# Moving the block transposes of an attention kernel from the tensor engine to crossbar DMAs

## The chip, the cores and the metric

One core of a Trainium2 chip. The metric is the device time of one execution in microseconds (us). Engines are called PE (matmul), DVE, ACT, POOL (GpSimd) and SP (the sync engine, which here only issues DMAs). All inputs and the result are float32 in HBM; the kernel computes in fp16. Three terms of the profile: the *granted clock* is the share of its full clock that PE was given (1.00 is all of it); a DMA *lands* when its data has arrived, and its landing time runs from its issue to then; a *crossbar DMA* is one that transposes its data on the way (`dma_start_transpose`).

## The reference

Block-sparse attention for 8 batches, 8 heads, 576 positions and a head width of 64, followed by a two-layer feed-forward product over the 4608 rows that result.

```python
scores = (1 / sqrt(D)) * q @ k.T
mask_local   = (rel >= 0) & (rel < 32)                   # heads 0..3
mask_strided = (rel >= 0) & (col % 32 == row % 32)       # heads 4..7
attn = softmax(where(mask, scores, -1e9)) @ v
x = attn.transpose(0, 2, 1, 3).reshape(4608, 512)
h = x @ w_in                                             # 512 -> 2048
out = (max(h, 0) + alpha * min(h, 0)) @ w_out            # 2048 -> 512
```

q and k are drawn with a standard deviation of 0.1. The scores are therefore close to zero and the softmax is nearly flat.

## The kernel before

The feed-forward part runs in 9 chunks of 512 rows. Each chunk has 16 pieces of the first product and 16 of the second, each piece four matmuls of 128x512. Between these pieces the attention of a later batch is fed in small pieces, so that PE always has a big matmul to go on with. A batch has four pairs of heads: pairs 0 and 1 local, 2 and 3 strided. A "unit" is two pairs (u even: local, u odd: strided). A "step" g of the schedule holds the scores of pair g, the product with v of pair g-1 and the transposed result of pair g-2.

q, k and the results must be transposed, and before the change PE does it, block by block against an identity, with an eviction by DVE or ACT:

```python
def transpose_piece(u, nm):                     # q or k of a unit
    tp = pspool.tile([128, 8, 64, 2], F16, ...)
    for j in range(8):
        keep(nc.tensor.transpose(tp[:, j]..., blk, ident))
    ...                                         # evict, then 2 or 4 more for the last 64 rows
def x_piece(P):                                 # the result of a pair
    xp = pspool.tile([128, 1024], F16, ...)
    for t in range(P.n):
        keep(nc.tensor.transpose(xp[...], P.x16[0:P.w, 128*t : 128*t+128], ident[...]))
    if P.strided: keep(nc.scalar.copy(xT[:, P.hp, ...], xp...))
    else:         keep(nc.vector.tensor_copy(xT[:, P.hp, ...], xp[:, 0:576]))
# step g:  S(g,0)  P(g-1,0)  T(q)  X(g-2)  S(g,1)  P(g-1,1)  T(k)  [P(g-1,2)]
```

A chunk's first product reads `xT`, the transposed results, so it can't start before the last result of its batch is in place. The transposes of q and k are needed before the scores of their unit.

The softmax here doesn't subtract the row's maximum and nothing guards it: scores larger than these inputs give would overflow.

## Time and profile before

| | before |
|---|---|
| time, median (range) | 343.4 us (343.15 to 343.47) |
| span of the profiled run | 341.7 us |
| PE busy, mean granted clock | 329.2 us (96%), 1.00 |
| matmul instructions | 2733 |
| packets on the software (POOL) DMA queue | 41,920 |
| packets on the hardware (SP) DMA queue | 8,768 |
| wait of PE for `xT` | 2.0 us, six times |

The busy share of PE says that PE bounds; the wait of PE for `xT` says where a chunk meets the attention that feeds it.

### The profile page before, as it was taken

To read this page: it belongs to the slowest core of one execution; us is meant where nothing else is said; L and a number is where in the kernel's file an instruction comes from. 1 tells how busy PE (TensorE), PEld (TensorE's weight loads), DVE (VectorE), ACT (ScalarE), POOL (GpSimd) and SP (SyncE) were. 2 spreads that over 40 slices of the span, in tenths; PEclk is the share of its full clock that TensorE was granted. 3 is DMA by queue.
4 is the path that set the end of the run, shared out by engine and by line. 5 is a ranking of instruction groups with operands and counts; after the bars stand their busy time and mean duration, and the time that the engine had idled before them with its cause. 6 is when DMAs were issued, how large, how long until landed. Compare 5 with 4: busy or idle time off the path is not lost.

```text
span 341.7 us, 6741 instructions
## 1 busy us (share of the span) xinstructions
PE 329.2 (96%) x2733; PEld 172.2 (50%) x2733; DVE 193.1 (57%) x385; ACT 175.7 (51%) x315; POOL 147.7 (43%) x164
## 2 busy tenths in 40 slices
PE   6899999999999999999999999999999999999995
PEld 2554455445554455454558754445545454444444
DVE  3477825489546863488247844784368446704800
ACT  2645664376356744474448544763467326524611
POOL 7832495339887257644575429122611210000000
PEclk9999999999999999999999999999999999999999
DMA  7999999398696472746366084000100010011011
GB/s 231 172 206 207 245 209 184 81 283 113 105 119 182 71 49 70 221 69 45 72 186 106 6 95 77 31 2 32 63 31 2 33 62 32 2 61 61 2 61 62
DMA packets 50719, 33.67 MB, mean 99 GB/s; under 512 B 31984, under 2 KB 42368, under 8 KB 50688
## 3 DMA queue, kind: packets, MB, share of 16 engines
q0 software_dynamic: 41920, 17.37, 42.7%
q1 hardware_dynamic: 8768, 15.87, 13.0%
q8 instruction: 21, 0.34, 0.4%
q14 instruction: 10, 0.08, 0.1%
HBM read 38.01 MB, written 9.44 MB: 139 GB/s over the span
## 4 chain that ended last, share of the span: by engine, by line
PE 90%; ACT 3%; DVE 3%; DMA 1%; issue 1%; SPq 0%; ACTq 0%
PE hps L493 36%; PE ops L535 35%; PE sp L271 4%; PE pv L318 4%; PE tp L214 4%; PE xp L335 2%; DMA ql<-in_q_dram 1%; PE wps L557 1%; DVE x L327 1%; PE ops L526 1%; ACT xT L339 1%; ACT osb L540 1%; PE sp L287 1%; PE sph L287 1%; ACT kT L159 1%
## 5 line engine op out<-in xcount | busy, mean ns | idle before, releaser
L535 PE MATMUL ops<-wout,gT 128*128 128x512 f16 x560 | 138.8, 379 | 0.0
L493 PE MATMUL hps<-xT,win 128*128 128x512 f16 (+1 forms) x640 | 135.2, 358 | 2.3 <-ACT xT L339 2.0
L506 DVE SCALAR_TENSOR_TENSOR gT<-neg,oma,hps 128x512 f16<-128x512 f32 x144 | 106.0, 744 | 47.3 <-ACT neg L503 39.5
L503 ACT ACTIVATE neg<-hps 128x512 f32<-128x512 f32 x144 | 86.0, 597 | 45.2 <-PE hps L493 44.4
L305 POOL TENSOR_TENSOR et<-et,consts 128x576 f16<-128x576 f16 (+1 forms) x48 | 61.1, 1275 | 88.6 <-ACT et L295 88.5
L493 PEld LDWEIGHTS <-win 128*128 128x128 f16 x640 | 58.8, 98 | 56.6 <-issue 4.8
L535 PEld LDWEIGHTS <-gT 128*128 128x128 f16 x560 | 48.2, 98 | 43.8
L540 ACT COPY osb<-ops 128x512 f32<-128x512 f32 x35 | 20.5, 585 | 67.1 <-PE ops L535 61.0
L325 DVE RECIPROCAL rc<-pv 72x6 f32<-72x6 f32 (+2 forms) x80 | 14.9, 186 | 58.7 <-PE pv L318 58.6
L295 ACT ACTIVATE et<-sp 72x576 f16<-72x576 f32 (+1 forms) x56 | 36.2, 647 | 21.5 <-PE sp L271 13.2
L327 DVE TENSOR_TENSOR x<-pv,rc 72x384 f16<-72x384 f32 (+2 forms) x80 | 42.2, 527 | 2.7
L318 PEld LDWEIGHTS <-et 72*128 72x128 f16 (+1 forms) x448 | 22.9, 98 | 15.4 <-DVE x L327 1.1
L271 PEld LDWEIGHTS <-kT 64*128 64x128 f16 x448 | 10.8, 95 | 27.3 <-issue 19.5
L161 DVE COPY qT<-tp 128x1024 f16<-128x1024 f16 (+1 forms) x16 | 17.4, 1086 | 8.0 <-PE tp L214 8.0
L271 PE MATMUL sp<-qT,kT 64*128 64x72 f16 (+1 forms) x392 | 16.9, 201 | 2.0 <-ACT kT L159 1.9
L159 ACT COPY kT<-tp 128x1024 f16<-128x1024 f16 (+1 forms) x16 | 14.5, 905 | 8.1 <-PE tp L214 8.1
L557 PE MATMUL wps<-wrm 128*128 128x512 f16 x44 | 15.2, 416 | 1.2 <-DVE wrm L569 1.2
L151 POOL DMA_DIRECT2D vl<-in_v_dram x8 | 11.2, 1403 | 10.8 <-PE xp L335 8.9
L335 PEld LDWEIGHTS <-x 72*128 72x128 f16 (+1 forms) x224 | 11.8, 97 | 7.9 <-DVE x L327 2.0
L318 PE MATMUL pv<-vs,et 72*128 72x65 f16 x256 | 15.1, 194 | 0.1
L335 PE MATMUL xp<-consts,x 72*128 72x72 f16 (+1 forms) x224 | 13.7, 200 | 1.0 <-DVE x L327 0.9
L163 POOL COPY vs<-stv 72x1024 f16<-72x1024 f16 x14 | 14.2, 1035 | 0.0
(66 smaller groups left out, 186.8 us busy)
## 6 DMA issues: line engine op xcount, KB each, us to landing
out_dram<-osb SPq DMA_DIRECT2D x35, 256.0 KB, 2.0
ql<-in_q_dram SPq DMA_DIRECT2D x6, 512.0 KB, 5.7
kl<-in_k_dram SPq DMA_DIRECT2D x6, 512.0 KB, 6.6
stv<-in_v_dram POOLq DMA_DIRECT2D x8, 288.0 KB, 6.4
vl<-in_v_dram POOLq DMA_DIRECT2D x6, 384.0 KB, 6.9
win<-in_moe_w_in_dram POOLq DMA_DIRECT2D x4, 512.0 KB, 10.4
wout<-in_moe_w_out_dram POOLq DMA_DIRECT2D x4, 512.0 KB, 18.1
qs<-in_q_dram POOLq DMA_DIRECT2D x7, 256.0 KB, 4.2
```

The costliest lines, as they stand in the source:

```text
L271: keep(nc.tensor.matmul(sps[y][:, w * x : w * x + w], P.kT[hf, k0 : k0 + 128], P.qT[hf, w * t : w * t + w], start=(x == 0), stop=(x == len ...
L295: keep(nc.scalar.activation(ev.rearrange("r (y c) -> r y c", y=2), sp[0:r, :, 0:n], AF.Exp, scale=SCALE))
L305: keep(nc.gpsimd.tensor_tensor(ev, ev, m, op=ALU.mult))
L318: keep(nc.tensor.matmul(pv[:, 65 * x : 65 * x + 65], et[0:r, c : c + 128], v16[0:r, 2 * P.pr + hh, t, :] if P.strided else v16[:, 6 * (2 * ...
L327: keep(nc.vector.tensor_tensor(P.x16[0:w, c0 : c0 + 64 * nb].rearrange("r (c e) -> r c e", e=64), pvv[:, :, 0:64], rc[0:w, 0:nb].unsqueeze ...
L335: keep(nc.tensor.transpose(xp[:, P.w * t : P.w * t + P.w], P.x16[0 : P.w, 128 * t : 128 * t + 128], ident[0 : P.w, 0 : P.w]))
L493: keep(nc.tensor.matmul(hps[:, dst : dst + w], win16[:, kk, 128 * m : 128 * m + 128], xT[:, kk, src : src + w], start=(kk == 0 and x == 0) ...
L503: keep(nc.scalar.activation(neg, hps, AF.Relu, scale=-1.0))
L506: keep(nc.vector.scalar_tensor_tensor(gTs[n][:, m, :], neg, oma[:, m : m + 1], hps, op0=ALU.mult, op1=ALU.add))
L535: keep(nc.tensor.matmul(ops, gTs[n][:, kf, 128 * mt : 128 * mt + 128], wout16[:, kf, :], start=(kf == 0), stop=(kf == 15)))
L540: keep(nc.scalar.copy(osb, ops))
L557: keep(nc.tensor.matmul(wps, wrm[:, 0:128], wrm, start=True, stop=True))
```

## The change

Intent: PE is the bound, and the transposes are PE work. From batch 3 on (`DX = 3`) they go to crossbar DMAs on the SP queue. The q and k that those read have to lie in SBUF as fp16: for strided heads in 72 rows of 8 positions, for local heads as overlapping row blocks of 96 and 128 rows, loaded with a cast by POOL's DMA queue. Results of local pairs go straight into `xT`; those of strided pairs into `xs`, from which ACT copies them in place. The diff, cut to its core:

```diff
+    DX = 3
+    def load_d(b, strided):                       # POOL queue, float32 -> fp16
+        for nm, src in (("q", q), ("k", k)):
+            if strided: keep(nc.gpsimd.dma_start(qks[nm][0:72], ...))        # 1 KB runs
+            else:       keep(nc.gpsimd.dma_start(qkl[nm], bass.AP(...        # 128 B runs
+                    ap=[[D, n], [96 * D, 24], [1, D]])))
+    def transpose_d(u):                           # SP queue
+        for nm, dst in (("q", qTs[u % 2]), ("k", kTs[u % 2])):
+            keep(nc.sync.dma_start_transpose(o, qks[nm]... or qkl[nm]...))
+    def x_dma(P):                                 # SP queue
+        if P.strided: P.xs = xpool.tile([128, 8, 80], F16, ...)
+                      keep(nc.sync.dma_start_transpose(P.xs, P.x16[0:80, :]))
+        else:         keep(nc.sync.dma_start_transpose(xT[:, P.hp, ...], P.x16[0:96, 0:768]))
+    def x_copy(P):
+        keep(nc.scalar.copy(xT[:, P.hp, ...], P.xs[:, :, 0:72].rearrange("r t p -> r p t")))
...                                                # in step g, c = g // 4
-        okT = 8 <= t < npair and t % 2 == 0
+        okT = 8 <= t < 4 * DX and t % 2 == 0
-        if okX: seq.append(("X", X(x), x))
+        if 8 <= g - 2 < 4 * DX: seq.append(("X", X(g - 2)))
+                if i == 0:
+                    if g % 4 == 2 and DX <= c + 1 < B:
+                        transpose_d(2 * (c + 1))
+                    if g % 4 == 0 and DX <= c < B:
+                        transpose_d(2 * c + 1)
+                        if c + 1 < B:
+                            load_d(c + 1, False)
+                    if g % 4 == 2 and DX <= c and c + 1 < B:
+                        load_d(c + 1, True)
                 for b, pr in extra:                # steps g % 4 == 0: v of this batch
                     cast_v(b, pr, "pool")
                     if pr == 1 and b + 1 < B:
                         load_v(b + 1, True)
+                if lastp:                          # after the last product with v of the step
+                    if 4 * DX <= g - 1 < npair:
+                        x_dma(pairs[g - 1])
+                if copyp and ... pairs[g - 2].strided:    # at the second scores of the step
+                    x_copy(pairs[g - 2])
...
-                acc += left / (23.5 - 0.5 * skip) * ...
+                acc += left / (22.0 - 0.5 * skip) * ...
```

The old loads, casts and tail loads of batches 3 to 7 are gone. In step g = 4c the strided transposes of batch c, the row-block loads of batch c+1 and the strided load of v for batch c+1 are issued; in step g = 4c + 2 the local transposes of batch c+1 and its strided loads of q and k. At the end of each step g the result of pair g-1 is transposed: in step g = 4c the last result of batch c-1, which the next chunk waits for.

More of the change, by code (lines that the diff above doesn't have):

```diff
@@ L85 @@
     NE = 6
-    qTs = [cpool.tile([128, 2, S], F16, name=f"qT{i}") for i in range(2)]
-    kTs = [cpool.tile([128, 2, 672], F16, name=f"kT{i}") for i in range(2)]
+    DX = 3
+    qTs = [cpool.tile([128, 2, 672], F16, name=f"qT{i}") for i in range(2)]
+    kTs = [cpool.tile([128, 2, 768], F16, name=f"kT{i}") for i in range(2)]
     vls = [cpool.tile([128, 24, 65], F16, name=f"vl{i}") for i in range(2)]
@@ L90 @@
     ets = [cpool.tile([128, 640], F16, name=f"et{i}") for i in range(NE)]
+    qkl = {nm: cpool.tile([128 if nm == "k" else 96, 24, 64], F16, name=f"{nm}ld") for nm in "qk"}
+    mloc = cpool.tile([128, 576], F16)
+    x16s = [cpool.tile([80, 1024], F16, name=f"x16s{i}") for i in range(2)]
+    qks = {nm: cpool.tile([80, 4, 512], F16, name=f"{nm}sd") for nm in "qk"}
     loaded = {}
@@ L112, in load_qk @@
             ap=[[8 * D, 64], [2 * S * D, 2], [S * D, 2], [1, 8 * D]])))
+    def load_d(b, strided):
+        for nm, src in (("q", q), ("k", k)):
+            if strided:
+                keep(nc.gpsimd.dma_start(
+                    qks[nm][0:72], src[b, 4:8, :, :].rearrange("h (p t) d -> p h (t d)", t=8)))
+            else:
+                n = 128 if nm == "k" else 96
+                base = src[b, 0:1, 0:1, :]
+                keep(nc.gpsimd.dma_start(qkl[nm], bass.AP(
+                    tensor=base.tensor, offset=base.offset - (n - 96) * D,
+                    ap=[[D, n], [96 * D, 24], [1, D]])))
+    def transpose_d(u):
+        for nm, dst in (("q", qTs[u % 2]), ("k", kTs[u % 2])):
+            flat = dst.rearrange("r e c -> r (e c)")
+            if u % 2:
+                o = flat[:, 0:1280].rearrange("r (j p) -> r j p", p=80)
+                keep(nc.sync.dma_start_transpose(o, qks[nm].rearrange("p h c -> p (h c)")))
+            else:
+                n = 128 if nm == "k" else 96
+                o = flat[:, 0 : 12 * n].rearrange("r (j p) -> r j p", p=n)
+                keep(nc.sync.dma_start_transpose(o, qkl[nm].rearrange("r w d -> r (w d)")))
     def cast_s(b, nm, eng):
@@ L192, in make_pair @@
         u = g // 2
-        P.qT, P.kT = qTs[u % 2][:, g % 2], kTs[u % 2][:, g % 2]
+        P.dx = P.b >= DX
+        if P.dx:
+            P.qT, P.kT = (z[u % 2].rearrange("r e c -> r (e c)") for z in (qTs, kTs))
+        else:
+            P.qT, P.kT = qTs[u % 2][:, g % 2], kTs[u % 2][:, g % 2]
         P.sgroups = ([0, 1, 2, 3], [4, 5, 6, 7]) if P.strided else ([0, 1, 2], [3, 4, 5])
@@ L208, in transpose_piece @@
         src = cast16[(b, strided, nm)]
-        dst = qTs[u % 2] if nm == "q" else kTs[u % 2][:, :, 32:608]
+        dst = qTs[u % 2][:, :, 0:576] if nm == "q" else kTs[u % 2][:, :, 32:608]
         tp = pspool.tile([128, 8, 64, 2], F16, tag="ps", name="tp")
@@ L243, in tails @@
                     tt[:, 128 * e : 128 * e + 128], tl[:, 128 * e : 128 * e + 128], ident))
-        for i, (o, eng) in enumerate(((qTs[u % 2], "dve"), (kTs[u % 2][:, :, 32:608], "act"))):
+        for i, (o, eng) in enumerate(((qTs[u % 2][:, :, 0:576], "dve"), (kTs[u % 2][:, :, 32:608], "act"))):
             if strided:
@@ L267, in score_piece @@
         for x, t in enumerate(grp):
-            k0 = 32 + 72 * t if P.strided else 96 * t
+            if P.dx and P.strided:
+                q0 = k0 = 80 * (4 * (2 * P.pr + t % 2) + t // 2)
+            elif P.dx:
+                j = 3 * (2 * P.pr + i) + x
+                q0, k0 = 96 * j, 128 * j
+            else:
+                q0, k0 = w * t, 32 + 72 * t if P.strided else 96 * t
             for y in range(2):
@@ L272, in score_piece @@
                     sps[y][:, w * x : w * x + w], P.kT[hf, k0 : k0 + 128],
-                    P.qT[hf, w * t : w * t + w], start=(x == 0),
+                    P.qT[hf, q0 : q0 + w], start=(x == 0),
                     stop=(x == len(grp) - 1 and not early), skip_group_check=True))
-                key = (2 * (t // 2) + y, t % 2) if P.strided else (t, y)
+                if P.dx and not P.strided:
+                    key = (2 * x + y, i)
+                else:
+                    key = (2 * (t // 2) + y, t % 2) if P.strided else (t, y)
                 P.et[key] = (et, n * y + w * x)
@@ L298, in score_piece @@
             return
-        if first:
+        if P.dx and not P.strided:
+            m = mloc
+        elif first:
             ev = ev.rearrange("r (y c) -> r y c", y=2)
@@ L308, in pv_piece @@
         if P.x16 is None:
-            P.x16 = xpool.tile([128, 1024], F16, tag="x16", name="x16")
+            if P.dx and P.strided:
+                P.x16 = x16s[P.pr]
+            else:
+                P.x16 = xpool.tile([128, 1024], F16, tag="x16", name="x16")
         v16 = cast16[(P.b, P.strided, "v")]
@@ L343, in x_piece @@
             keep(nc.vector.tensor_copy(xT[:, P.hp, base : base + S], xp[:, 0:576]))
+    def x_dma(P):
+        base = (P.b % 4) * S
+        if P.strided:
+            P.xs = xpool.tile([128, 8, 80], F16, tag="xs", bufs=2, name="xs")
+            keep(nc.sync.dma_start_transpose(P.xs, P.x16[0:80, :]))
+        else:
+            keep(nc.sync.dma_start_transpose(
+                xT[:, P.hp, base : base + S].rearrange("r (w p) -> r w p", p=96), P.x16[0:96, 0:768]))
+    def x_copy(P):
+        base = (P.b % 4) * S
+        keep(nc.scalar.copy(
+            xT[:, P.hp, base : base + S].rearrange("r (p t) -> r p t", t=8),
+            P.xs[:, :, 0:72].rearrange("r t p -> r p t")))
     npair = 4 * B
@@ L407 @@
     for g in range(7, npair + 2):
-        a, p, t, x = g, g - 1, g + 1, g - 2
+        c = g // 4
+        a, p, t = g, g - 1, g + 1
         okA = 8 <= a < npair
         okP = 8 <= p < npair
-        okT = 8 <= t < npair and t % 2 == 0
-        okX = 8 <= x < npair
+        okT = 8 <= t < 4 * DX and t % 2 == 0
         nP = len(pairs[p].pgroups) if okP else 0
@@ L415 @@
         if okA:
-            seq.append(("S", Sc(a, 0), a))
+            seq.append(("S", Sc(a, 0)))
         if okP:
-            seq.append(("P0", Pv(p, 0), p))
+            seq.append(("P", Pv(p, 0)))
         if okT:
-            seq.append(("T", T(t // 2, "q"), t))
-        if okX:
-            seq.append(("X", X(x), x))
+            seq.append(("T", T(t // 2, "q")))
+        if 8 <= g - 2 < 4 * DX:
+            seq.append(("X", X(g - 2)))
         if okA:
-            seq.append(("S", Sc(a, 1), a))
+            seq.append(("S2", Sc(a, 1)))
         if okP:
-            seq.append(("P", Pv(p, 1), p))
+            seq.append(("P", Pv(p, 1)))
         if okT:
-            seq.append(("Tk", T(t // 2, "k"), t))
+            seq.append(("T", T(t // 2, "k")))
         if nP == 3:
-            seq.append(("P", Pv(p, 2), p))
-        todo = [(g // 4, pr) for pr in range(2)] if g % 4 == 0 and 8 <= g < npair else []
-        if g % 4 == 1 and 9 <= g and g // 4 + 1 < B:
-            todo = [(g // 4 + 1, nm) for nm in "qk"]
-        lastP = max([i for i, s in enumerate(seq) if s[0][0] == "P"], default=-1)
-        nslots = [i for i, s in enumerate(seq) if s[0] != "S"] or list(range(len(seq)))
-        for i, (kind, fn, gg) in enumerate(seq):
+            seq.append(("P", Pv(p, 2)))
+        if not seq:
+            seq.append(("N", lambda: None))
+        todo = [(c, pr) for pr in range(2)] if g % 4 == 0 and 8 <= g < npair else []
+        lastP = max([i for i, z in enumerate(seq) if z[0] == "P"], default=len(seq) - 1)
+        copyP = next((i for i, z in enumerate(seq) if z[0] == "S2"), 0)
+        nslots = [i for i, z in enumerate(seq) if z[0][0] != "S"] or list(range(len(seq)))
+        for i, (kind, fn) in enumerate(seq):
             extra = []
@@ L443, with run @@
                 extra = [todo.pop(0) for _ in range(min(cnt, len(todo)))]
-            def run(fn=fn, extra=extra, u=t // 2, kind=kind, g=g, lastp=(i == lastP)):
+            def run(fn=fn, extra=extra, g=g, c=c, i=i, lastp=(i == lastP), copyp=(i == copyP)):
                 fn()
-                for b, pr in extra:
-                    if pr in ("q", "k"):
-                        cast_l(b, pr)
-                        if b + 1 < B:
-                            load_qk(b + 1, False, pr)
-                        continue
+                if i == 0:
[7 more added lines that the diff above has]
+                        load_d(c + 1, True)
+                for b, pr in extra:
                     cast_v(b, pr, "pool")
@@ L455, in run @@
                         load_v(b + 1, True)
-                if kind == "Tk" and u // 2 + 2 < B:
-                    if u % 2 == 1:
-                        load_qk(u // 2 + 2, True, "q")
-                        load_qk(u // 2 + 2, True, "k")
-                    load_tail(u // 2 + 2, u % 2 == 1)
-                if lastp and g % 4 == 2 and g // 4 + 2 < B:
-                    load_v(g // 4 + 2, False)
-            feed(run, gg if kind == "X" else -1)
+                if lastp:
+                    if 4 * DX <= g - 1 < npair:
+                        x_dma(pairs[g - 1])
+                    if g % 4 == 2 and c + 2 < B:
+                        load_v(c + 2, False)
+                if copyp and 4 * DX <= g - 2 < npair and pairs[g - 2].strided:
+                    x_copy(pairs[g - 2])
+            if g - 2 >= 4 * DX:
+                feed(run, g - 2 if i == copyP else -1)
+            else:
+                feed(run, g - 2 if kind == "X" else -1)
     pos = {"i": 0}
@@ L569 @@
     keep(nc.vector.memset(wrm, 0.0))
+    for nm in "qk":
+        keep(nc.vector.memset(qks[nm][64:80], 0.0))
+    for t in x16s:
+        keep(nc.vector.memset(t[64:80], 0.0))
     keep(nc.sync.dma_start(consts, consts_dram))
@@ L650 @@
     wide["on"] = False
-    load_unit(3, False)
-    load_unit(3, True, False)
+    load_d(3, False)
+    keep(nc.gpsimd.tensor_copy(mloc[:, 0:288], mfirst))
+    keep(nc.gpsimd.tensor_copy(mloc[:, 288:480], consts[:, 224:416]))
+    keep(nc.gpsimd.tensor_copy(mloc[:, 480:576], mother))
+    load_v(3, False)
+    load_d(3, True)
     for n in range(1, NCH):
@@ L665 @@
             if i >= skip:
-                acc += left / (23.5 - 0.5 * skip) * (0.5 if i < 16 else 1.0)
+                acc += left / (22.0 - 0.5 * skip) * (0.5 if i < 16 else 1.0)
             cnt = int(acc)
```

## The prediction

> **What bounds the kernel now.** I read the page's busy shares first, then its chain of waits, then the stretches of time of the steady part, then the timeline of the tensor engine alone.
>
> ```profile
> PE 329.2 (96%) x2733; PEld 172.2 (50%) x2733; DVE 193.1 (57%) x385; ACT 175.7 (51%) x315; POOL 147.7 (43%) x164
> ...
> PE 90%; ACT 3%; DVE 3%; DMA 1%; issue 1%; SPq 0%; ACTq 0%
> ```
>
> The tensor engine (PE) is busy for 96% of the span and carries 90% of the chain that ended last; no other engine passes 57%. That alone doesn't say what a removed PE instruction is worth, so I looked at the stretches. Each holds about one chunk of 512 rows of the two large products plus one batch of attention; the columns after the length are busy times of PE, weight loads, DVE, ACT and POOL, then clock, DMA share and GB/s.
>
> ```profile
> 134.00:172.00 38.00, 37.65 (x330) 19.05 (x329) 22.54 (x45) 21.18 (x38) 22.30 (x23) 1.00 0.51 92
> 172.00:212.00 40.00, 39.77 (x407) 26.37 (x405) 23.66 (x48) 21.17 (x37) 22.69 (x22) 1.00 0.54 94
> 212.00:248.00 36.00, 35.65 (x308) 18.05 (x307) 21.93 (x44) 20.00 (x35) 13.18 (x12) 1.00 0.10 36
> 248.00:284.00 36.00, 35.27 (x274) 17.22 (x273) 19.52 (x40) 18.71 (x33) 6.36 (x5) 1.00 0.10 38
> ```
>
> PE idles 0.2 to 0.7 us per stretch at a full clock. So it is issue-bound here: what is taken off PE comes off the time, provided nothing new makes it wait. The one recurring wait is at the start of a chunk, for the last piece of the attention result:
>
> ```profile
> PE hps L493 <- ACT xT L339: 2.0, 6, 0.3
> ```
>
> Six waits of 0.3 us, one per chunk. That is where the change can hurt, because it puts a DMA into exactly that path.
>
> **What the Trainium skill says.** (1) "Trainium Kernel Development and Optimization", Performance Expectations: matmul busy time is a poor metric because matmuls are pipelined. The trace agrees: the 64 transposes of one operand have records of 219 ns each but only 4.9 us in union, and even that overstates them, as shown next. (2) "TensorE: Matmul & The Clock Gate", Part 4: a PE transpose of 128x128 takes about 390 ns alone and about 275 ns in a kernel. Here the record is 219 ns and eight in a row delay the next product by only 0.45 us, 56 ns each; the trace decides. (3) "DMA: Bandwidth & Descriptors", Latency and other measured facts: a DMA transpose runs at 261 GB/s with a non-contiguous middle dimension and at 350 to 400 otherwise. The kernel before has no such DMA, so no run yet shows it; I size the transfers with 261. (4) The same page, Anatomy of one DMA: about 2 us fixed for a DMA, there for the GpSimd path. The plain stores from the sync queue land 256 KB in 2.0 us here, so I take 2 us as a ceiling for the fixed part.
>
> ```profile
> out_dram<-osb SPq DMA_DIRECT2D x35, 256.0 KB, 2.0
> ...
> vl<-in_v_dram POOLq DMA_DIRECT2D x6, 384.0 KB, 6.9
> ```
>
> **What it removes from PE.** Instruction count first: the build has 660 fewer PE rows, which is 330 weight loads and 330 matmuls. Per batch that is 8+8 block transposes for the strided unit with 4 for its tail, 8+8 for the local unit with 2, and 6+6+8+8 for the results: 66; five batches (3 to 7) make 330. For their price I compare start times on PE, where a group of four products with nothing behind it takes 0.86 us to the next start:
>
> ```profile
> 210.00 1.03 PE L535 MATMUL ops<-wout,gT 128*128 128x512 f16 x4
> 210.86 0.61 PE L214 MATMUL tp<-consts,qs 128*128 128x128 f16 x8
> 211.31 1.03 PE L535 MATMUL ops<-wout,gT 128*128 128x512 f16 x4
> 212.17 0.42 PE L335 MATMUL xp<-consts,x 72*128 72x72 f16 x8
> 212.43 0.81 PE L493 MATMUL hps<-xT,win 128*128 128x512 f16 x3
> 213.59 1.24 PE L493 MATMUL hps<-xT,win 128*128 128x512 f16 x5 [0.35 <-ACT xT L339]
> ...
> 218.65 0.61 PE L214 MATMUL tp<-consts,ks 128*128 128x128 f16 x8
> 219.19 0.29 PE L237 MATMUL tt<-consts,tl 64*128 64x64 f16 x4
> 219.41 1.90 PE L493 MATMUL hps<-xT,win 128*128 128x512 f16 x8
> ...
> 236.31 0.61 PE L214 MATMUL tp<-consts,kl 128*128 128x128 f16 x8
> 236.76 0.28 PE L242 MATMUL tt<-consts,tl 128*128 128x128 f16 x2
> 236.87 1.03 PE L535 MATMUL ops<-wout,gT 128*128 128x512 f16 x4
> ```
>
> So q of the strided unit costs 211.31 - 210.86 = 0.45 us, its k with the tail 219.41 - 218.65 = 0.76, the local q 0.45 (a group like the first), the local k with its tail 236.87 - 236.31 = 0.56, and each result 212.43 - 212.17 = 0.26, four times 1.04. The sum is 3.26 us per batch. Times five: **16.3 us**. The busy sums would have said 23.6 us (5/8 of 19.6 for the blocks, 4.5 for the tails and 13.7 for the results); I reject that, since union time counts pipeline overlap with the products around.
>
> A cross-check: the starts of consecutive chunks lie 35.9 us apart (177.69, 213.59, 249.46 in the chain). 128 products of 0.2156 us make 27.6; scores (eight groups at 0.24 plus 0.10 at the change of operand) 2.7; products with v about 1.7; transposes 3.26; the start wait 0.35. Sum 35.6, so the price list is complete to 0.3 us. Without transposes I expect chunks of about **32.5 us**.
>
> **What it takes from the other engines.** DVE loses two large evictions (1.2 us) with small ones and two copies (0.45 us) per batch, ACT two evictions (1.0 us) with small ones; ACT keeps two copies of the strided results (0.65 us), now from SBUF. POOL loses two casts (1.04 us each) and four tail issues (0.55 to 0.69 us), and gains two row-block loads whose issue should cost about what the load of v costs, 1.48 us. None bounds, so I count all this as zero.
>
> **What it adds.** Per batch the sync queue gets four transposes of q, k (393, 295 and 2 x 328 KB, by the tile sizes) and four of results (147 and 164 KB, two each): 2.0 MB, by 261 GB/s some 7.5 us of transfer per 32.5 us. The q, k of local heads come in 5,376 packets of 128 B in place of 512 of 2 KB and the tails; the load of v has the same form with 3,072 and lands in 6.9 us. Each of these loads is issued about half a batch, 16 us, before its transpose, and each transpose of q, k two pairs, again 16 us, before its scores. All of that is beside the path.
>
> **What lies on the path** is the last result of a batch. Its transpose is issued after the last product with v; three pieces later ACT copies it into place. At the new pacing (18 pieces per batch over 22 weighted slots, 0.82 per slot) three pieces are 3.7 slots of about 1.15 us, 4.2 us; ACT gets there about 1 us later, and DVE needs about 1.2 us to make the tile. That leaves 4.0 us for the DMA. By my estimate it needs 2 + 164 KB/261 GB/s = 2.6 us. Ahead of it in the queue stand the two 328 KB transposes issued four pieces, 4.9 us, earlier; they need 2 + 2 x 1.25 = 4.5 us. So it fits with about 1 us to spare, after which two slots (the new divisor 22.0 against 24 weighted slots) remain before the next chunk needs it. Only batch 7 is tight: with no scores left, one piece lies between issue and copy. There the chain is 1.2 + 2.6 + 0.65 = 4.5 us against some 4.1, so up to 1 us of waiting. I allow 1.5 us in all for new waits.
>
> Sum: 343.4 - 16.3 + 1.5 = **328.6 us**.
>
> **Rivals.** (a) *The crossbar wait replaces the transposes.* If the transposes are two to three times slower than 261 GB/s, or hold the queue while they run, the 328 KB pair ends 2 to 8 us late and the last result with it; ACT, in order, then stands before the copy and PE runs out of tiles. Each us beyond the slack costs 5 us over five batches: 2 us late gives about 338, 4 us late 348. For it: no such DMA is in this trace and eight of them per batch go through one queue with the stores. Against: the sync queue is nearly empty now (some six issues per batch of 0.3 to 0.6 us), and the slots have evidently been moved for slack. (b) *The evictions or POOL become the bound.* At 32.5 us per chunk DVE would be at about 60% and ACT below 60%; nothing in the windows speaks for it. If it held, the gain would be halved, 335. (c) *The small packets crowd the DMA engines.* From 96 to 212 us their share is already 0.5 to 0.6, and the loads of v push it over 2 for 2 us; a transpose caught behind such a load could land 3 to 5 us late. The engines are almost empty after 212 us before the change, but now the last two loads of q, k fall later. Where it strikes the last result it costs as in (a), in one or two batches: 331 to 336. (d) *More than counted*: the start waits of 0.35 us go as well, about 325.5.
>
> **Range and chances.** The removal is measured well; the spread is nearly all in (a) and (c). I give the clean case with small waits 65%, (c) or a mild (a) at 331 to 336.5 20%, a strong (a) 15%. Range 324.5 to 337.0. Faster by over 2% means below 336.5: 0.84; same 0.11; slower 0.05.
>
> **What would show it.** Right: chunk starts 32.3 to 33 us apart, 2403 matmuls with PE still at 95% or more, transposes landing in 2.5 to 4 us, waits of ACT for the copy of the strided result below 1 us each. Wrong: transposes landing after 6 us or issued late because the sync queue is held; ACT waiting several us before that copy; PE waiting for xT at each chunk start by over 1 us; or scores waiting for the transposed q and k.

## More of the kernel before

The lines of the page are in the prediction. Three more are needed later. The first is the busy share of the DMA engines in 40 slices of the span, in tenths. The second is the group of ACT copies that put a strided result in place (least, median and greatest duration in ns). The third is from the chain of waits in order of time: nine matmuls of a chunk's start, the yardstick for a PE at full clock.

```profile
DMA  7999999398696472746366084000100010011011
...
L339 ACT COPY xT<-xp x16: 638/645/672, 22.5 to 282.2; 128x576 f16<-128x576 f16 x16
...
249.46 2.10 PE hps L493 x9
```

## The result, and the profile after

The changed kernel takes 354.4 us (353.5 to 357.5), the kernel before 343.4: ratio 1.034, interval 1.029 to 1.039. It is slower, by about as much as it was forecast to be faster. (A ratio here is the mean time of one kernel's fast runs over that of the other's of the same rounds, so it is not quite the ratio of the medians quoted.) A run more than 1.5% above the fastest of its kernel is called slow and left out of the ratio.

The page of the changed kernel, in order: busy shares, busy tenths of PE, its granted clock and the DMA engines' share in 40 slices, and the chain that ended last by engine.

```profile
PE 323.7 (91%) x2403; PEld 160.0 (45%) x2403; DVE 178.8 (50%) x354; ACT 170.9 (48%) x290; POOL 140.6 (40%) x147
...
PE   7899999999969999399956999499999997999995
...
PEclk9999999999998999789996999879999999999999
DMA  7999999937994999869993999946450122011012
...
PE 76%; DMA 10%; POOL 4%; ACT 3%; DVE 3%; issue 1%; SPq 1%; POOLq 0%; ACTq 0%
```

The 330 matmuls are gone as counted (2733 - 330 = 2403). But PE's row now has holes, with a fall of the granted clock in each, and a tenth of the last chain is DMA time. The packets rise from 41,920 to 66,080 on POOL's queue and from 8,768 to 45,728 on SP's, and the DMA engines, before the change mostly at 2 to 8 tenths from the 10th slice to the 25th, are at 9 tenths in most of these slices. The waits of PE name the hole (total us, times, longest):

```profile
PE hps L566 <- ACT xT L407: 20.1, 4, 7.1
PE pv L369 <- POOL et L353: 2.9, 1, 2.9
```

The first is the start of a chunk waiting for the last result. The chain in order of time (start, us, what) shows one such place as cause and effect:

```profile
137.04 9.28 DMA xs<-x16s
146.34 1.31 ACT xT L407
147.70 4.00 PE hps L566 x9
```

A crossbar transpose of 164 KB is under way for 9.28 us, then ACT copies for 1.31 us, then PE starts, and needs 4.00 us for nine matmuls that took 2.10 before the change. So each hole is paid twice. The timeline of the two issuing engines at that place gives what else was under way (SP first, then POOL; start, us, what):

```profile
131.24 1.28 SPq L141 DMA_TRANSPOSE qT<-qsd  x1
132.61 2.67 SPq L141 DMA_TRANSPOSE kT<-ksd  x1
...
137.04 1.37 SPq L400 DMA_TRANSPOSE xs<-x16s  x1
```

```profile
132.65 1.24 POOL L130 DMA_DIRECT2D qld<-in_q_dram  x1
133.88 1.44 POOL L130 DMA_DIRECT2D kld<-in_k_dram  x1
...
138.52 0.80 POOL L176 DMA_DIRECT2D stv<-in_v_dram  x1
```

Ahead of the result in its own queue stand two large transposes of q and k; from the other queue come the row blocks of q and k in small packets (128 B in the trace), and v. Either could be the cause. The row blocks and the transposes come from the change; the load of v stood at this step before it.

The step of the last batch is a first hint. There the last result of batch 6 has the same two transposes ahead (batch 7's q and k), but nothing is left to load. The SP timeline there:

```profile
254.15 1.35 SPq L141 DMA_TRANSPOSE qT<-qsd  x1
255.59 1.93 SPq L141 DMA_TRANSPOSE kT<-ksd  x1
...
259.20 1.21 SPq L400 DMA_TRANSPOSE xs<-x16s  x1
```

The ten strided results of the changed kernel land in 3.2, 9.3, 2.7, 10.5, 2.7, 8.5, 2.7, 2.7, 2.7 and 2.7 us: slow are exactly the last results of batches 3, 4 and 5, the three that meet loads. (A last result is every second number; that of batch 5 was issued at 219.3 us, that of batch 6 at 259.2.)

**The account.** The span grew by 355.7 - 341.7 = 14.0 us. Off PE went 16.3 us, as priced. Added were 20.1 - 2.0 = 18.1 us of waiting for `xT` (6.1, 7.1 and 5.0 at the three slow results, 1.9 at batch 7's last), and 2.9 us of waiting for POOL's masks. Half-clock matmuls after the four long holes make the rest. After each hole at a chunk start the first nine matmuls (or seventeen of half width) take 3.8 to 4.0 us in place of 2.0 to 2.1, and the next group is slower by 0.2 to 0.9 us: 7.4 us in three holes. After the wait for the masks eight matmuls take 2.79 us and the next twelve 3.59, where groups of that size take 1.90 and 2.75 elsewhere: 1.7 us. The sum is -16.3 + 18.1 + 2.9 + 7.4 + 1.7 = 13.8 us. The half-clock stretch behind the wait for masks is not there in every execution: in e4 the same wait of 2.9 us left the clock at 1.00, and the next four matmuls took their usual 1.03 us.

### The profile page after: what moved, and what is told of

Same layout as the page of the kernel before. It is cut to its first block, busy times and chain, and to the rows that moved or that the text cites. A ratio compares the mean times of both kernels' runs of the same rounds, so it can differ in the third digit from the quotient of the medians.

```text
span 355.7 us, 6091 instructions
## 1 busy us (share of the span) xinstructions
PE 323.7 (91%) x2403; PEld 160.0 (45%) x2403; DVE 178.8 (50%) x354; ACT 170.9 (48%) x290; POOL 140.6 (40%) x147
## 3 DMA queue, kind: packets, MB, share of 16 engines
q0 software_dynamic: 66080, 20.49, 59.4%
q1 hardware_dynamic: 45728, 20.46, 28.3%
## 4 chain that ended last, share of the span: by engine, by line
PE 76%; DMA 10%; POOL 4%; ACT 3%; DVE 3%; issue 1%; SPq 1%; POOLq 0%; ACTq 0%
PE hps L566 37%; PE ops L608 27%; DMA xs<-x16s 9%; PE pv L369 3%; PE sp L314 3%; POOL et L353 2%; ACT xT L407 1%; DMA ql<-in_q_dram 1%; PE wps L630 1%; DVE x L378 1%; PE tp L251 1%; PE ops L599 1%; PE sph L333 1%; PE sp L333 1%; ACT kT L192 1%
## 5 line engine op out<-in xcount | busy, mean ns | idle before, releaser
L566 PE MATMUL hps<-xT,win 128*128 128x512 f16 (+1 forms) x640 | 141.4, 374 | 20.4 <-ACT xT L407 20.1
L608 PE MATMUL ops<-wout,gT 128*128 128x512 f16 x560 | 137.1, 381 | 0.0
L566 PEld LDWEIGHTS <-win 128*128 128x128 f16 x640 | 62.4, 102 | 82.7 <-issue 30.1
L353 POOL TENSOR_TENSOR et<-et,consts 72x576 f16<-72x576 f16 (+1 forms) x28 | 35.5, 1271 | 96.1 <-ACT et L341 96.1
L341 ACT ACTIVATE et<-sp 72x576 f16<-72x576 f32 (+1 forms) x56 | 36.2, 647 | 36.1 <-PE sp L314 26.5
L353 POOL TENSOR_TENSOR et<-et,mloc 128x576 f16<-128x576 f16 x20 | 25.3, 1276 | 21.2 <-ACT et L341 21.1
L378 DVE TENSOR_TENSOR x<-pv,rc 96x384 f16<-96x384 f32 (+2 forms) x50 | 26.9, 538 | 1.7
L407 ACT COPY xT<-xs 128x576 f16<-128x576 f16 x10 | 13.0, 1304 | 25.7 <-DMA xs<-x16s 25.7
L314 PE MATMUL sp<-qT,kT 64*128 64x72 f16 (+1 forms) x392 | 16.9, 201 | 2.0 <-ACT kT L192 1.9
L630 PE MATMUL wps<-wrm 128*128 128x512 f16 x44 | 16.4, 449 | 1.2 <-DVE wrm L642 1.2
L378 DVE TENSOR_TENSOR x16s<-pv,rc 72x384 f16<-72x384 f32 (+1 forms) x30 | 15.3, 509 | 1.0
L369 PE MATMUL pv<-vl,et 128*128 128x65 f16 x192 | 12.0, 199 | 2.9 <-POOL et L353 2.9
## 6 DMA issues: line engine op xcount, KB each, us to landing
kld<-in_k_dram POOLq DMA_DIRECT2D x5, 384.0 KB, 11.4
kl<-in_k_dram POOLq DMA_DIRECT2D x3, 512.0 KB, 10.9
```

What stands on the lines that cost most here:

```text
L314: keep(nc.tensor.matmul(sps[y][:, w * x : w * x + w], P.kT[hf, k0 : k0 + 128], P.qT[hf, q0 : q0 + w], start=(x == 0), stop=(x == len(grp) ...
L341: keep(nc.scalar.activation(ev.rearrange("r (y c) -> r y c", y=2), sp[0:r, :, 0:n], AF.Exp, scale=SCALE))
L353: keep(nc.gpsimd.tensor_tensor(ev, ev, m, op=ALU.mult))
L369: keep(nc.tensor.matmul(pv[:, 65 * x : 65 * x + 65], et[0:r, c : c + 128], v16[0:r, 2 * P.pr + hh, t, :] if P.strided else v16[:, 6 * (2 * ...
L378: keep(nc.vector.tensor_tensor(P.x16[0:w, c0 : c0 + 64 * nb].rearrange("r (c e) -> r c e", e=64), pvv[:, :, 0:64], rc[0:w, 0:nb].unsqueeze ...
L407: keep(nc.scalar.copy(xT[:, P.hp, base : base + S].rearrange("r (p t) -> r p t", t=8), P.xs[:, :, 0:72].rearrange("r t p -> r p t")))
```

## The experiments

Each run was timed in three rounds against the kernel before, which stayed between 343.1 and 343.6 us. **A caution on "correct"**: all twelve runs passed the comparison with the reference, also those that use the wrong q and k. With scores this near to zero the comparison doesn't see q and k, so it vouches for v, masks and order of results, not for them; that the repaired versions use the right ones rests on their code.

Landing times are read in the profiled runs; those of e1 and e5 are slow ones.

| run | edit | median us | ratio | last result of batches 3, 4, 5 lands in (us) |
|---|---|---|---|---|
| changed kernel | | 354.4 | 1.034 | 9.3, 10.5, 8.5 |
| e1 | local row blocks loaded once | 341.0 | (see text) | 7.0, 6.7, 7.0 |
| e2 | strided q, k transposed once | 338.6 | 0.986 | 6.4, 5.6, 5.1 |
| e6 | both | 334.3 | 0.974 | 6.4, 6.4, 5.7 |
| e11 | e1, and v's load moved | 328.4 | 0.956 | 4.1, 4.3, 2.7 |
| e3 | row blocks loaded and transposed a step later | 346.9 | 1.007 | 6.2, 5.6, 5.4 |
| e4 | all results on PE | 337.3 | 0.983 | none |
| e5 | all loads and q, k transposes moved | 353.9 | (see text) | 9.5, 5.2, 6.5 |
| e7 | e5, all results on PE | 336.2 | 0.979 | none |
| e8 | e5, last result on PE | 334.6 | 0.974 | none |
| e12 | strided results on PE, row blocks loaded earlier | 329.2 | 0.959 | none |
| e13 | last result on PE | 330.1 | 0.961 | none |
| e14 | e13, row blocks loaded behind the masks | **326.5** | **0.951** | none |

### Which cost is it? e1, e2, e6, e11

Theory A: loads from the POOL queue hold up the transpose. Theory B: the two q, k transposes ahead of it in the SP queue do.

**e1**, the row-block loads for batch 3 only:

```diff
                         transpose_d(2 * c + 1)
-                        if c + 1 < B:
-                            load_d(c + 1, False)
```

> The row-block loads of local q and k are issued for batch 3 only; later batches transpose batch 3's rows again (wrong result on purpose, all transposes and waits stay). Theory A (the 5,376 small packets of these loads, issued at the same step as the last result's transpose, hold it up on the DMA engines): the last strided result lands in 2.7 to 4 us in place of 8.5 to 10.5, PE's wait for xT falls from 20 us to under 3, time 326 to 332. Theory B (the result's transpose stands behind the two strided q, k transposes in the same queue): it still lands in 6 us or more and the time stays above 345.

Three of its four runs (340.8 to 341.6 us) are slow against its fastest, 335.6; the profiled one is of these. So no ratio is given, and its landing times carry no weight here beyond this: neither theory's number came out. Something is left that neither names.

**e2**, the strided transposes for batch 3 only:

```diff
-                        transpose_d(2 * c + 1)
+                        if c == DX:
+                            transpose_d(2 * c + 1)
```

> The two crossbar transposes of strided q and k run for batch 3 only (wrong result on purpose); all loads and all result transposes stay. Theory A (small-packet loads): the last result still lands in 6 to 9 us because the loads are still there, time 345 to 353. Theory B (order in the queue behind these two): it lands in about 2.7 us, time 326 to 332.

338.6 us, ratio 0.986 (0.982 to 0.991). With the two transposes gone after batch 3 the last results still land in 5.1 to 6.4 us, at or below the low end of A's 6 to 9 and far from B's 2.7, but the time fell below A's range: PE's wait for `xT` is 7.4 us in place of 20.1, and without long holes the clock is 0.990 to 0.995 in place of 0.965 to 0.971.

**e6**, both edits at once:

> Both removals at once: row-block loads and strided q, k transposes for batch 3 only (wrong result on purpose). A+B: the last result lands in 2.7 to 4 us, PE waits under 3 us for xT, time 326 to 331. C: it still takes over 5 us and the time stays near that of the single removals, 338 to 341.

334.3 us, ratio 0.974 (0.968 to 0.981), runs 332.6 to 337.3. The time lies between the two forecasts. C (the result's transpose is slow there for another reason, such as stores or v's load; it is set out under e5) has its sign come out: the last results land in 5.7 to 6.4 us, with no row blocks loaded and (after batch 3) no strided transposes ahead. What remains at this place is the load of v for the next batch, issued at step 4c as before the change: 288 KB, cast, on the POOL queue.

**e11** tests this: e1's edit, and v's load a step later, with both q, k transposes left ahead of the result.

```diff
                     cast_v(b, pr, "pool")
-                    if pr == 1 and b + 1 < B:
-                        load_v(b + 1, True)
...
                 if lastp:
+                    if g % 4 == 1 and 8 <= g and c + 1 < B:
+                        load_v(c + 1, True)
```

> As the run with rows loaded once (wrong result on purpose), and v's strided load moves from the first to the second step of a batch, behind the copy of the last result: no load from the GpSimd queue is then under way at that place, while both strided q, k transposes still stand ahead of the last result in the sync queue. Theory A' (any load under way there is what delays the transpose; the queue order costs nothing, as the last batch's 2.7 us already suggests): all strided results land in 2.6 to 3.5 us, no wait of PE for xT over 1.2 us, time 327 to 330. Theory B (queue order): the last result still takes 5 us or more and the time stays above 335.

328.4 us (327.7 to 328.8), ratio 0.956 (0.955 to 0.958). Landing times of the ten strided results, and PE's wait for them:

```profile
DMA to landing us min/median/max: 2.6/2.7/5.8
...
PE hps L564 <- ACT xT L407: 2.6, 3, 1.9
```

B as the main cause is refuted: the two transposes are still ahead, and the last results land in 4.1, 4.3, 2.7, 2.7 and 2.6 us. A' isn't met in full either: one landing takes 5.8 us and one wait 1.9 (batch 7's, which the changed kernel has too), and at the 4.1 and 4.3 us no load of the POOL queue is under way in the trace; what slowed these two is open. What delays the others is a load under way on the POOL queue; v's alone, in packets of 1 KB, is enough (e6). Row blocks without v's load at this place were not run.

The landing times say which load it is. Of the changed kernel, e2, e3 and e6, each of the twelve slow last results lands within 0.8 us of a load that was under way: k's row blocks in the changed kernel and e2, v's in e3 and e6. Here is the landing time of k's row blocks for batch 5, in the changed kernel (issued at 133.9 us) and in e2 (issued at 134.0):

```profile
DMA to landing us min/median/max: 12.9/12.9/12.9
...
DMA to landing us min/median/max: 8.4/8.4/8.4
```

So in the changed kernel they land at 146.8 us, and the result, issued at 137.04, at 146.3. This also says how the q, k transposes matter only in company: with them ahead, k's row blocks take 11.4 to 13.8 us to land at this place, without them (e2) 7.1 to 8.4, and the last result comes in with the row blocks both times, after 8.5 to 10.5 or after 5.1 to 6.4 us. Without loads they cost at most 1.6 us (4.3 against 2.7 in e11), and nothing in batch 7's step of the changed kernel. That the times coincide is read from the traces; why the transpose ends with the load is not shown.

e11 also shows the removal to be worth what it was priced at: with the loads away the time is 328.4, and 328.6 had been predicted, though this run leaves out loads that a right kernel needs.

### Moving the collision: e3, e5

**e3** moves the row-block loads behind the copy of the last result, and their transposes a step later too.

```diff
-                    if g % 4 == 2 and DX <= c + 1 < B:
+                    if g % 4 == 3 and DX <= c + 1 < B:
                         transpose_d(2 * (c + 1))
-                        if c + 1 < B:                       # at g % 4 == 0, i == 0
-                            load_d(c + 1, False)
+                    if g % 4 == 1 and DX <= c and c + 1 < B:   # at lastp
+                        load_d(c + 1, False)
```

> Right result. The row-block loads of local q and k move from the first piece of the batch to the end of its second step, after the last result of the batch before is in place, and the transposes that read them move one step later as well. Theory A: results land in 2.7 to 4 us, PE's wait for xT under 3 us, POOL no longer late with its masks, time 327 to 332. Theory B: the last result still lands in over 6 us, time above 345.

346.9 us, ratio 1.007. The last results still land in 5.4 to 6.2 us, since v's load stayed where it was. And there is a miss by my own edit: the results' wait fell to 7.6 us, but one step of lead is too little for k, and scores now wait for it:

```profile
PE sp L314 <- DMA kT<-kld: 10.8, 4, 5.8
```

**e5** moves everything out of that stretch: a third pair of transposed buffers, q and k loaded two batches ahead (conditions shortened; the fp16 tiles of strided q and k of the earlier batches also go from three buffers to two).

```diff
+    def slot(u):                      # which of three qT, kT buffers
+        return 0 if u % 2 == 0 else 1 + u // 2 % 2
                 if i == 0:
+                    g % 4 == 2: transpose_d(2 * (c + 1) + 1)
+                    g % 4 == 3: load_d(c + 2, True)
                 if lastp:
+                    g % 4 == 1: transpose_d(2 * (c + 1)); load_v(c + 1, True)
+                    g % 4 == 2: load_d(c + 2, False)
```

> Right result. Every load and every transpose of q and k is moved out of the stretch between the second last result of a batch and the copy of its last one (a third pair of transposed buffers, loads two batches ahead, v's strided load moved as well). Theory A+B (both the small-packet loads and the two q, k transposes delay the last result, each by 3 to 4 us, and POOL's masks are late behind the issue of the loads): last result in 2.7 to 3.5 us, PE's wait for xT under 3 us in all, clock back at 1.00, time 327 to 331. Theory C (a result's transpose is slow at that place for another reason, such as the output stores or v's load): still over 5 us, time above 340.

353.9 us; three of four runs slow against a fastest of 347.8, so no ratio. The window is not quiet. In the profiled run (a slow one) the row blocks and the strided q, k take medians of 8.7 to 12.9 us from issue to landing, and the first strided result of a batch, which ACT also waits for, now meets loads: it lands in 10.9 to 13.4 us for batches 3 to 5, and PE waits 17.4 us for ACT behind it. The loads were moved off one transfer that something waits for and onto another.

### Taking the transpose off the path: e4, e7, e8, e12, e13, e14

**e4**: q and k stay on the crossbar, all results go back to PE, with the old pacing (`x_dma` and `x_copy` dropped, `X` for all pairs, 23.5).

> Right result. q and k stay on the crossbar, the attention results go back to PE transposes with the old pacing. PE then saves 2.22 us per batch in place of 3.26, 11 us in all: 332 if the path of the last result is the only place where the change loses (theories A and B alike). If the time is above 336, there is another loss, such as POOL's late masks (2.9 us) or scores that wait for their transposed q and k.

337.3 us, ratio 0.983 (0.981 to 0.984). No wait for a transpose is left (PE waits 2.0 us for `xT`, as before the change), yet 5 us are missing to the price. PE waits 4.0 us for POOL's masks, and 2.7 us in place of 1.9 for `kT`, which together make 4.8 of these 5 us. So there is a second loss, and it is nearly all masks.

**e7** is e5's placing of loads with e4's results:

> Right result. The moved loads and transposes of the quiet window, with all results transposed on PE at the old pacing. If the 5 us that the version with results on PE lacked (337.3 in place of the priced 332) come from POOL's masks standing behind the issue of the row-block loads, this gives 331 to 334 and PE's wait for POOL falls below 1 us; if from something else, it stays at 336 to 338.

336.2 us, ratio 0.979. The time lies in the second range, but the wait for masks is 2.1 us, not below 1, so the first was not put to the test. The trace still accounts for the 4 us above the price: after a wait for masks of 1.9 us the clock halves (four matmuls take 1.90 us in place of 1.03, the next twelve 3.18 in place of 2.75: 1.3 us), the waits for masks make 2.1, and `kT` again 0.8 more than before.

**e8** is e5 with only the last result on PE:

> Right result. The quiet window, with only the last result of each batch transposed on PE, the other three by the crossbar. PE saves 3.0 us per batch and no DMA is on the path into the next chunk: 328 to 331 by A+B, and not more than 1 us from the quiet window itself if that one really has no wait left; clearly faster than it if the crossbar's 2.7 us plus the 1.3 us copy still hold PE up.

334.6 us, ratio 0.974, 13 us below e5's fastest run by one result of four. That speaks for the path; but with PE waiting 4.5 us for masks it misses its range, as POOL's loads now stand in front of them elsewhere.

**e13** is the smallest repair: the changed kernel, with the last result of each batch on PE.

```diff
-        if 8 <= g - 2 < 4 * DX:
+        if 8 <= g - 2 < npair and (g - 2 < 4 * DX or g % 4 == 1):
             seq.append(("X", X(g - 2)))
-                    if 4 * DX <= g - 1 < npair:
+                    if 4 * DX <= g - 1 < npair and g % 4:
                         x_dma(pairs[g - 1])
-                if copyp and ... and pairs[g - 2].strided:
+                if copyp and ... and g % 4 == 0:
                     x_copy(pairs[g - 2])
```

> Right result. The smallest repair: only the last result of each batch goes back to a PE transpose, everything else is as in the changed kernel. If the loss is all on that one transpose (A' and B alike), PE's 20 us of waits for xT and the half-clock stretches vanish; left are POOL's late masks (3 to 5 us): 332 to 335. If it stays above 340, the reading of the path is wrong.

330.1 us (329.1 to 331.0), ratio 0.961 (0.958 to 0.963): 24 us below the changed kernel, though this edit gives 5 x 0.26 = 1.3 us of transposes back to PE. All loads and all other transposes are still there. This places the loss: not the DMAs as such, but one of eight transposes per batch standing on the path while loads run. PE no longer waits for `xT` at all. The spans fit the account: they differ by 355.7 - 329.2 = 26.5 us, and the waits of 20.1 us and the 7.4 us behind them, less the 1.3, make 26.2. What the list of waits still has is the mask, 2.9 us once, as in the changed kernel. The time lies below its range.

**e12** puts both strided results on PE (the condition `g % 4 < 2` for X, `1 <= g % 4 <= 2` for `x_dma`, no `x_copy`) and issues the row-block loads at the end of step 4c - 1.

> Right result. Both strided results of a batch go back to PE (0.52 us per batch dearer), local ones stay on the crossbar, and the row-block loads are issued one step earlier, so that they don't stand before POOL's masks at the first step of a batch. Priced by PE alone: 343.4 - 5 x 2.74 = 329.7. A': 330 to 333, with neither ACT nor PE waiting for a transpose. If it stays above 335, loads and POOL still cost elsewhere.

329.2 us, ratio 0.959, just below its range and within 0.5 us of its PE price. PE waits 2.1 us for a mask.

**e14** is e13 with the row-block loads issued behind the casts and masks of their step:

```diff
                         transpose_d(2 * c + 1)
-                        if c + 1 < B:
-                            load_d(c + 1, False)
                 if lastp:
+                    if g % 4 == 0 and DX <= c and c + 1 < B:
+                        load_d(c + 1, False)
```

> Right result. As the run with the last result on PE, with the row-block loads issued at the end of the first step of a batch, behind the masks and casts of that step. If POOL's late masks are what is left, this is 3 to 4 us faster than that run, 329 to 332, and PE's wait for POOL falls below 1 us; if the loads now land too late, PE waits for kT instead and the time is 333 or more.

326.5 us (326.4 to 326.5), ratio 0.951 (0.949 to 0.952). It beats both kernels. Its wait for masks, busy shares and chain:

```profile
PE pv L369 <- POOL et L353: 0.3, 1, 0.3
...
PE 315.0 (97%) x2443; PEld 158.1 (49%) x2443; DVE 178.5 (55%) x354; ACT 168.4 (52%) x290; POOL 140.6 (43%) x147
...
PE 91%; DVE 3%; ACT 2%; DMA 1%; POOL 1%; issue 1%; SPq 0%; ACTq 0%
```

The loads take 2.7 us to issue on POOL (1.25 and 1.43 us), and in the changed kernel they stood before the casts and the masks that the next product with v needs. Behind the mask they cost PE 0.3 us: 3.6 us between e13 and e14, as was forecast, though the time itself lies below its range, as e13's did. Up to 1.5 of the 3.6 us is clock: two of e13's four runs were at 0.995 (330.7 and 331.0 us), two at 1.00 (329.1 and 329.5). PE again carries 91% of the chain, with 290 fewer matmuls than before, which were priced at 5 x 3.0 = 15.0 us; measured are 16.9, the start waits of 2.0 us having gone as well.

## Why the prediction was wrong, point by point

**Right:** that PE bounds, and what the removed transposes are worth. 16.3 us by start times, not the 23.6 of the busy sums, is confirmed by e11 (15 us gained, with 2.6 us of waits for results left and 1.3 for k), e12 (14.2 against 13.7) and e14 (16.9 against 15.0).

**Right:** where it could hurt. "The one recurring wait is at the start of a chunk ... it puts a DMA into exactly that path." The 20.1 us lie there.

**The step that failed** is in "What lies on the path": "By my estimate it needs 2 + 164 KB/261 GB/s = 2.6 us", "so it fits with about 1 us to spare". Alone the transpose does take 2.7 us. But the estimate was for idle DMA engines, and at this place three loads from the other queue are issued around it; it took 8.5 to 10.5 us in three of five batches. The loads had been judged by their own deadlines alone ("All of that is beside the path"). PE's list shows no wait for them, so they weren't late; they were in the way. The Trainium skill's "DMA: Bandwidth & Descriptors", Issuing engines are not separate DMA queues, says that DMAs run on the same 16 engines "and interleave with each other, regardless of the engine that started them", and e11 against e6 agrees: v's load alone makes 2.7 to 4.3 us into 5.7 to 6.4.

**Rival (c) named the cause and was mis-sized.** It put a transpose behind a load 3 to 5 us late, in one or two batches, 331 to 336 us. It was 6 to 8 us later than alone, in three batches, since the schedule issues these loads at this very step of every batch that has a successor. It named small packets; v's load, in packets of 1 KB, was enough. Reading where `load_d`, `load_v` and `x_dma` stand in the step would have told how often they meet.

**Two smaller sizes in the same sum were off.** The copy by ACT was put at 0.65 us, as from PSUM, and took 1.30 from SBUF. The two q, k transposes ahead were put at 4.5 us and took 6.2 even with no load under way (batch 7's, 254.15 to 260.3 us). The result itself landed in 2.7 us there, yet PE waited 1.9 us, in e11 too, where up to 1 had been foreseen; the copy explains 0.65 of it.

**A term that was missing:** the clock. A hole of several us is followed by matmuls at half speed, 9.1 us in all by the account. The prediction charged each us of lateness once. "TensorE: Matmul & The Clock Gate", Why this matters for your kernels, warns of it: no PE-idle gaps over about 3 us. I had looked at that page for the transposes only. No length of wait alone decides it in these runs, though: waits of 1.9 us (e7) and 2.9 (changed kernel) were followed by half speed, one of 2.9 (e4) was not.

**A second term wrongly set to zero:** POOL. "None bounds, so I count all this as zero" was by busy share. But in the timeline above POOL's work follows one behind the other: the issues of the row blocks run from 132.65 to 135.3 us and the next mask comes after them. 2.7 us of issue in front of a mask that PE needs soon is a matter of place, not of share: 2.9 us of waiting, 3.6 us from e13 to e14.

**Rival (a)** (a slow crossbar, or a queue held by the transposes) came nearest in size, 4 us late giving 348 (measured 354), but for another reason. **Rival (b)** didn't occur. The check "transposes landing after 6 us" was the right thing to look for.

Open: by what means a load holds a crossbar transpose up until it lands itself; how far the size of packets matters; what the row blocks do without v's load; the 4.1 and 4.3 us of e11. The pacing (23.5 in e4 and e7, 22.0 elsewhere) was never varied alone.

## What to carry to other kernels

Before moving work from a busy engine to DMA, find the one transfer that something waits for, and list what every queue issues in the few us around it: a time measured or estimated on idle engines doesn't hold there. Leave that one transfer on the engine (here 1.3 us in all) and move the rest: e13 turned a loss of 3.4% into a gain of 4%. And where an engine's work runs one piece behind the other, as POOL's does here, put the issue of loads behind whatever the bounding engine will need next.

## What the Trainium skill lacked or had wrong

- "DMA: Bandwidth & Descriptors" says in Rules for kernel authors that "A transpose next to ordinary DMAs needs nothing". That is about correctness. It lacks the cost: a crossbar transpose of 164 KB landed in 2.7 us alone, in 5.7 to 6.4 us beside one load of 288 KB, and in 8.5 to 10.5 us beside row-block loads, v's load and two more transposes.
- "TensorE: Matmul & The Clock Gate" gives about 3 us (elsewhere 3.4 us) of idling before the clock halves. Here a wait of 2.9 us (for the masks) was enough in the changed kernel, where the next eight matmuls took 2.79 us in place of 1.90, and one of 1.9 us in e7; in e4 one of 2.9 us was not. So these figures are no safe limit for one wait.
- The same page, Part 4, gives 275 ns for a PE transpose within a kernel. Eight in a row cost 56 ns each here (0.45 us by start times), for records of 219 ns; Part 4 doesn't say that transposes pipeline, though the page's Part 1 measures 55 to 56 ns between matmuls of this width at full clock, which is what fits here.
- No page gives these two durations: ACT's copy of a strided result took 1.30 us from SBUF (elements 160 bytes apart) and 0.645 us from PSUM (144 bytes apart) for the same 128x576 fp16 elements. The runs don't separate memory from step.
